# Pooled attention and a gated feed-forward net: the odd 64 query rows of two heads share one pass of the product with v

## The chip, the cores and the metric

The kernel runs on one core of a Trainium2 chip. A core has a matrix engine (PE, with its weight loads shown apart as PEld), a vector engine (DVE), an activation engine (ACT), a general engine (POOL) and a queue that issues transfers (SP). PE writes to a small accumulator memory (PSUM, eight banks of 512 float32 columns on 128 partitions); the other data lie in on-chip memory of 128 partitions. The metric is the device time of one execution in microseconds (us), lower is better; each of the times below is one execution.

## What is computed

There are 8 batches of 8 heads, 1152 keys and a head size of 64. Pairs of neighbouring query rows are averaged first, so a head has 576 query rows. The heads' outputs stand side by side as x (576 rows of 512 in a batch), and x goes through a net that mixes each row with the row before it:

```python
q_pool = q.reshape(B, H, S // 2, 2, D).mean(axis=3)
scores = scale * np.matmul(q_pool, k.transpose(0, 1, 3, 2))
scores = scores - np.max(scores, axis=-1, keepdims=True)
attn = np.exp(scores)
attn = attn / (np.sum(attn, axis=-1, keepdims=True) + 1e-09)
attn_out = np.matmul(attn, v)
# x: the heads side by side; x_prev: the row before, zeros ahead of the first
xk = mu_k * x + (1.0 - mu_k) * x_prev
xr = mu_r * x + (1.0 - mu_r) * x_prev
k = np.maximum(xk @ w_k, 0.0)          # 512 -> 1024
v = k * k @ w_v                        # 1024 -> 512
r = 1.0 / (1.0 + np.exp(-(xr @ w_r)))  # 512 -> 512
return r * v
```

The inputs are float32, the three weight matrices float64; the kernel splits numbers into a high and a low float16 part and sums products of the parts.

## The kernel before

**Attention.** A head's 576 query rows go in six blocks of 96 (`block`). For a block, nine PE products (L528) make the scores of 128 keys by 96 rows each in one of three PSUM buffers `s`; DVE takes the largest over the key chunks (`mx`, L535), PE turns it round (L538), DVE reduces it to one number per row (`mb`, L541), PE spreads its negative over a row (L543), and ACT writes that row, scaled a little up or down by its sign (Prelu), as row 96 of the low query parts (`qT`, L546). Nine more products (L552) then add the low parts and, through that row, subtract the maximum. ACT takes the exponential (`pf`, L558), an int32 whose upper half is the high part; POOL makes the low part from the lower half (`pl`, L566).

**The product with v.** `window` takes 128 of a head's rows as PE's stationary operand and v as the moving one: nine key chunks of `pf` against the parts of v (`vt`), then nine of `pl` (`vb`). 576 is four and a half times 128, so there are five windows per head, at rows 0, 128, 256, 352 and 448 (`WIN`), and the last ones overlap. Column 64 of v is ones, so that each result carries the row's sum. For the first 8 heads each chunk of `pf` meets the high and the low half of v in two products of 65 and 64 columns that add up in PSUM (L592, L594). From head 8 on (`SPLIT`) one product of 129 columns makes both halves side by side (L589), windows are taken out in two groups of three and two, and the halves are added afterwards: ACT copies one (`xlb`, L620), DVE adds it (L622). DVE also takes the sum (L615), its reciprocal (L617) and the scaled result (`xb`, L624). All of it lies in one PSUM bank, `a`, so the next group of windows begins when the one before it has been read. After every second head `xb` is turned round in five PE transposes (L636) and ACT copies it in two pieces to `xt` (L639).

**The net.** `ff` runs over tiles of 256 rows of x: mixing on ACT and DVE (L748, L751, L756, L759), then PE products of 256 or 512 columns (L780). The net of a batch can begin when its heads are done, so PE has it beside the attention of the next batch, and the last batch's net stands alone at the end. In the first batch there is no net yet; instead the weights are decoded on ACT, DVE and POOL (L657 to L691).

**What sets the order.** Every step is recorded as an `op` with engine, duration, what it reads and writes, and a key. `Issue` plays the steps through (list scheduling, with latencies `LAT`, `ISSUED`, `LANDED`), disturbs the priorities by a table of numbers (`MOVES`), and then issues them in the order found. On the chip each engine works through its own list in that order.

The lines of the change: `queries` loads and sums the query rows (L421, L423), `block` has the row of the maximum, `window` all of the product with v.

## Time and profile before

| | |
|---|---|
| median of three executions | 1159.55 us (1158.46 to 1159.95) |
| profiled execution, its own time | 1160.88 us |
| its span in the trace | 1159.1 us |
| granted PE clock, mean | 0.993 |
| busy: PE, DVE, ACT, POOL | 1115.5, 946.5, 917.6, 515.0 us |

The profile's page gives the busy time of each engine, 40 slices of the span, the chain of work that ended last and the costliest groups of instructions. A group's row names the line, the engine, the operation, output and inputs with their shapes, and how often it occurs; then the busy time, the mean of one in ns, and the idle time of the engine before it with what ended it. The timeline has one row for a run of equal instructions: start, length, and in brackets the idle time before it. A PE product's length counts from its start to its end in PSUM and overlaps with the next one's, so what a product occupies of PE is read from the distance of the starts. The view by windows gives the engines' busy time in a stretch of the span.

### The profile page before, as it was taken

To read this page: it belongs to the slowest core of one execution; us is meant where nothing else is said; L and a number is where in the kernel's file an instruction comes from. 1 tells how busy PE (TensorE), PEld (TensorE's weight loads), DVE (VectorE), ACT (ScalarE), POOL (GpSimd) and SP (SyncE) were. 2 spreads that over 40 slices of the span, in tenths; PEclk is the share of its full clock that TensorE was granted. 3 is DMA by queue.
4 is the path that set the end of the run, shared out by engine and by line. 5 is a ranking of instruction groups with operands and counts; after the bars stand their busy time and mean duration, and the time that the engine had idled before them with its cause. 6 is when DMAs were issued, how large, how long until landed. Compare 5 with 4: busy or idle time off the path is not lost.

```text
span 1159.1 us, 40985 instructions
## 1 busy us (share of the span) xinstructions
PE 1115.5 (96%) x17012; PEld 922.0 (80%) x17012; DVE 946.5 (82%) x2093; ACT 917.6 (79%) x1963; POOL 515.0 (44%) x541
## 2 busy tenths in 40 slices
PE   6787799999999999999999999999999999999998
PEld 5776787878788887988787888878797878788565
DVE  8888988889988979897888888887988987775531
ACT  7998897887878787887977877878888777866743
POOL 3555554644444444544444444445453544543111
PEclk9998899999999999999999999999999999999999
DMA  8877755553544434454454544354455433310000
GB/s 223 216 179 182 153 115 138 134 123 105 125 119 101 124 92 103 108 117 100 113 131 100 114 97 114 93 122 104 107 115 113 105 81 88 72 27 4 26 20 28
DMA packets 218667, 125.48 MB, mean 108 GB/s; under 512 B 153968, under 2 KB 190832, under 8 KB 218480
## 3 DMA queue, kind: packets, MB, share of 16 engines
q1 hardware_dynamic: 218480, 122.85, 44.9%
q8 instruction: 133, 2.18, 0.8%
q14 instruction: 54, 0.44, 0.1%
HBM read 67.11 MB, written 9.44 MB: 66 GB/s over the span
## 4 chain that ended last, share of the span: by engine, by line
PE 74%; ACT 7%; DVE 4%; issue 2%; DMA 0%; SPq 0%; ACTq 0%; DVEq 0%
PE f L780 30%; PE a L589 10%; PE s L528 9%; PE s L552 9%; PE a L599 5%; PE s L780 4%; ACT pf L558 2%; DVE mx L535 2%; PE a L780 2%; PE s L538 2%; PE a L636 1%; PE s L543 1%; ACT qT L546 1%; ACT qn L426 1%; ACT kn L474 0%
## 5 line engine op out<-in xcount | busy, mean ns | idle before, releaser
L566 POOL TENSOR_SCALAR pl<-pf 128x864 f16<-128x864 uint16 x384 | 374.1, 974 | 472.0 <-ACT pf L558 445.2
L535 DVE TENSOR_REDUCE mx<-s 128x96 f16<-128x864 f32 x384 | 400.8, 1052 | 69.2 <-PE s L528 40.7
L558 ACT ACTIVATE pf<-s 128x864 int32<-128x864 f32 x384 | 337.5, 891 | 70.2 <-PE s L552 45.7
L528 PE MATMUL s<-qT,ks 128*128 128x96 f16 x3456 | 225.0, 208 | 11.5 <-ACT pf L558 9.9
L528 PEld LDWEIGHTS <-ks 128*128 128x128 f16 x3456 | 189.9, 99 | 43.9 <-issue 19.4
L552 PE MATMUL s<-qT,ks 128*128 128x96 f16 x3456 | 218.9, 207 | 3.2 <-ACT qT L546 2.1
L589 PE MATMUL a<-vt,pf 128*128 128x129 f16 x2520 | 210.9, 220 | 0.5 <-DVE xb L624 0.5
L552 PEld LDWEIGHTS <-ks 128*128 128x128 f16 x3456 | 184.6, 99 | 26.9 <-issue 6.3
L589 PEld LDWEIGHTS <-pf 128*128 128x128 f16 x2520 | 159.6, 98 | 10.8 <-issue 0.6
L599 PE MATMUL a<-vb,pl 128*128 128x65 f16 x2880 | 151.2, 193 | 0.0
L546 ACT ACTIVATE qT<-s 1x96 f16<-1x96 f32 x384 | 92.0, 243 | 69.5 <-PE s L543 59.9
L780 PE MATMUL f<-xhk,wk_hi 128*128 128x256 f16 x496 | 135.1, 272 | 0.3 <-ACT r L807 0.3
L780 PE MATMUL f<-xhk,wk_lo 128*128 128x256 f16 x496 | 135.1, 272 | 0.0
L780 PE MATMUL f<-xlk,wk_hi 128*128 128x256 f16 x496 | 135.1, 272 | 0.0
L599 PEld LDWEIGHTS <-pl 128*128 128x128 f16 x2880 | 124.7, 98 | 3.6 <-POOL pl L566 0.2
L541 DVE TENSOR_REDUCE mb<-s 96x1 f16<-96x128 f32 x384 | 107.2, 282 | 22.9 <-PE s L538 18.9
L811 POOL TENSOR_TENSOR gl<-g 128x512 f16<-128x512 f32 x72 | 77.9, 1082 | 107.9 <-ACT g L809 105.2
L780 PEld LDWEIGHTS <-wk_hi 128*128 128x128 f16 x1152 | 107.0, 98 | 11.3 <-issue 0.4
L780 PE MATMUL f<-wv_hi,g 128*128 128x512 f16 x240 | 90.9, 379 | 0.9 <-ACT ex L828 0.7
L538 PE MATMUL s<-identb,mx 128*96 128x128 f16 x384 | 86.1, 226 | 5.4 <-DVE mx L535 5.2
L780 PE MATMUL f<-wv_hi,gl 128*128 128x512 f16 x240 | 90.9, 379 | 0.0
L780 PE MATMUL f<-wv_lo,g 128*128 128x512 f16 x240 | 90.9, 379 | 0.0
(106 smaller groups left out, 1976.9 us busy)
## 6 DMA issues: line engine op xcount, KB each, us to landing
kr<-in_k_dram SPq DMA_DIRECT2D x64, 288.0 KB, 3.0
vr<-in_v_dram SPq DMA_DIRECT2D x64, 288.0 KB, 3.0
qr<-in_q_dram SPq DMA_DIRECT2D x31, 320.0 KB, 3.6
ks<-ks SPq DMA_DIRECT2D x64, 144.0 KB, 2.8
out_dram<-em SPq DMA_DIRECT2D x36, 256.0 KB, 2.5
qr<-in_q_dram SPq DMA_DIRECT2D x32, 256.0 KB, 3.3
st<-in_moe_w_k_dram SPq DMA_DIRECT2D x8, 512.0 KB, 4.9
st<-in_moe_w_v_dram SPq DMA_DIRECT2D x8, 512.0 KB, 4.1
```

The source lines that it names most:

```text
L528: nc.tensor.matmul(cols(c, c + 1), ks1[hp][:, c, :], qhi, start=(c == c0), stop=False, skip_group_check=True)
L535: op("DVE", 0.975, lambda: nc.vector.tensor_reduce(mxz, grid(0, NC).rearrange("p c q -> p q c"), axis=AX.X, op=ALU.max), r=[("s", z)], w=[ ...
L538: op("PE", 0.059, lambda: nc.tensor.matmul(s[0:QN, 0:P], mxz, identb, start=False, stop=False, skip_group_check=True), r=[("mx", z)], w=[( ...
L541: op("DVE", 0.199, lambda: nc.vector.tensor_reduce(mbz[0:QN], s[0:QN, 0:P], axis=AX.X, op=ALU.max), r=[("s", z)], w=[("mb", z)], key=t + O ...
L546: op("ACT", 0.153, lambda: nc.scalar.activation(qlo[QN:QN + 1], s[QN:QN + 1, 0:QN], AF.Prelu, scale=1.0 - EPS, alpha=(1.0 + EPS) / (1.0 - ...
L552: nc.tensor.matmul(cols(c, c + 1), ks2[hp][:, c, :], qlo, start=False, stop=True, skip_group_check=True)
L558: op("ACT", NC * QN / 1200 + 0.06, lambda: nc.scalar.activation(pf[:, :, rows], grid(0, NC), AF.Exp, bias=SHIFT, scale=0.125 / (2.0 * SQ)) ...
L566: op(pe, d, lambda: en.tensor_scalar(pl[:, :, rows], half(pf, U16, 0)[:, :, rows], LO, 1.0, op0=ALU.mult, op1=ALU.mult), r=[("pf", j)], w= ...
L589: nc.tensor.matmul(bank[:, a0:a0 + VN + D], half(pf, F16, 1)[:, c, rows], vt[jv][:, c, 0:VN + D], start=(w == k0 and c == 0), stop=False, ...
L599: nc.tensor.matmul(bank[:, a0 + two * D:a0 + two * D + VN], pl[:, c, rows], vb[jv][:, c, 0:VN], start=False, stop=(c == NC - 1), skip_grou ...
L780: nc.tensor.matmul(ps, terms[i][0], terms[i][1], start=(first and i == 0), stop=(i == last), skip_group_check=True)
L811: op("POOL", 2 * n * 0.00203 + 0.08, lambda f2=f2: nc.gpsimd.tensor_tensor(gl[:, f2, 0:n], g32[:, f2, 0:n], gh[:, f2, 0:n], op=ALU.subtrac ...
```

## The change

The query rows of two neighbouring heads (an even one and the odd one after it) are laid out anew: the first 64 rows of both lie in one shared chunk, and the other 512 rows of each head make four windows of 128 without overlap. The exponentials of the even head's 64 rows lie at the end of `pf` and `pl` (which grow by 64), those of the odd head at the beginning. A new function `halves` runs once per two heads: for each chunk two products whose stationary operand has only 64 columns, one writing partitions 0 to 63 of bank `a` (even head, its v) and one partitions 64 to 127 (odd head, its v); the program gives them PE tiles of 128 rows by 64 columns at column 0 and column 64. Whole windows always use the two products that add up in PSUM, so the 129-column form, `SPLIT` and the copy and add per group of windows are gone; they remain for the shared pass alone. A head's windows are taken out together, four for the even head, four and the shared pass for the odd one. POOL copies the odd head's part of the shared result beside the even one's; the transposed results go to `xt` in four ACT copies, two of them of 64 columns on 64 partitions.

The row of the maximum becomes two rows: ACT writes Relu(x) and Relu(-x) with a scale that is a column of numbers (`sign`), and rows 96 and 97 of `ks2` hold the two factors; `EPS` doubles. DVE makes `sign` and `lift` and scales the two `ks2` at the start; POOL makes `negd`, which only a variant that isn't chosen (`row == "D"`) uses. The queries of two heads come in one transfer more. The planner's table `MOVES`, its seed's spread, some latencies and loads are other ones, so the order differs everywhere.

```diff
-EPS = 2.0 ** -10
+EPS = 2.0 ** -9
+ROW, ROW_N = "AA", 0
...
-SPLIT = 8
+HALF = 1.1
...
-    5, 10, 11, 17, 73, 89, 126, 158, 244, 307, 353, 431, 520, 523, 545, 560, 575, 593, 721, 784, 789, 846,
...
+    12, 57, 71, 78, 82, 116, 127, 165, 204, 389, 459, 497, 555, 573, 765, 911, 920, 1257, 1370, 1565, 1944,
...
-    LAT = {("PE", "DMA"): 1.46, ("PE", "PE"): 0.0,
+    LAT = {("PE", "DMA"): 0.2, ("PE", "PE"): 0.0,
...
-    ISSUED, LANDED, AHEAD = 1.44, 0.52, 8.0
+    ISSUED, LANDED, AHEAD = 1.2, 0.45, 8.0
...
-        return self.LAT.get((a, b), 1.22 if b == "DMA" else 0.18)
+        return self.LAT.get((a, b), 0.14 if b == "DMA" else 0.18)
...
-    WIN = [(0, 1), (128, 2), (256, 3), (352, 4), (448, 5)]
-    NW = len(WIN)
-    TURN = [(0, 3, 0), (3, 5, 384)]
+    HW, U = P // 2, 32
+    DONE = ((1, 2, 3, 5), (1, 3, 4, 5))
+    NW = 1 + len(DONE[0])
+    TURN = [(0, 3), (3, NW)]
+    SPAN = [(0, HW), (0, HW), (HW, HW + 2 * P), (HW + 2 * P, TQ)]
...
+    sign, lift = const.tile([P, 1], F32, name="sign"), const.tile([P, 1], F32, name="lift")
+    for c_, a_, b_ in ((sign, -2.0, 1.0), (lift, -2.0 * SM, SM * (1.0 - EPS))):
+        nc.vector.tensor_scalar(c_, ident[:, QN + 1:QN + 2], a_, b_, op0=ALU.mult, op1=ALU.add)
...
-        nc.vector.memset(t_[QN:QN + 1], SM)
+        nc.vector.memset(t_[QN:QN + 2], 1.0)
+        nc.vector.tensor_scalar(t_[QN:QN + 2], t_[QN:QN + 2], lift[QN:QN + 2], None, op0=ALU.mult)
...
-        op("ACT", 0.153, lambda: nc.scalar.activation(qlo[QN:QN + 1], s[QN:QN + 1, 0:QN], AF.Prelu,
-                                                      scale=1.0 - EPS, alpha=(1.0 + EPS) / (1.0 - EPS)),
-           r=[("s", z)] + kl, w=qm, key=t + O_MAX)
...
+                op("ACT", 0.267, lambda: nc.scalar.activation(qlo[QN:QN + 2], s[QN:QN + 2, 0:QN], AF.Relu,
+                                                              scale=sign[QN:QN + 2]),
+                   r=[("s", z)] + kl, w=qm, key=t + O_MAX)
...
+    def halves(n, t):
...
+        def both(r0, tb, c, vs, x0, x1, **kw):
+            for z, p0 in ((0, TQ), (1, 0)):
+                nc.tensor.matmul(a_b[z * HW:(z + 1) * HW, x0:x1], tb[:, c, p0:p0 + HW], vs[(n - 1 + z) % NV][:, c, r0:r0 + x1 - x0],
+                                 skip_group_check=True, **kw)
+
+        def mms():
+            for c in range(NC):
+                both(0, half(pf, F16, 1), c, vt, 0, place(0) + VN, start=(c == 0), stop=False)
+            for c in range(NC):
+                both(0, pl, c, vb, place(0), place(0) + VN, start=False, stop=(c == NC - 1))
...
+        x_ = xl_b[0]
+        op("ACT", 0.051 + D / 1200, lambda: nc.scalar.copy(x_, a_b[:, 0:D]), r=[ka], w=[("xlb",)], key=t + O_EVAC)
+        op("DVE", 0.07 + D / 960, lambda: nc.vector.tensor_tensor(
+            a_b[:, D:2 * D], a_b[:, D:2 * D], x_, op=ALU.add), r=[ka, ("xlb",)], w=[ka], key=t + O_EVAC)
...
-                if two:
-                    nc.tensor.matmul(bank[:, a0:a0 + VN + D], half(pf, F16, 1)[:, c, rows], vt[jv][:, c, 0:VN + D],
-                                     start=(w == k0 and c == 0), stop=False, skip_group_check=True)
-                    continue
...
+        op("POOL", 0.2, lambda: nc.gpsimd.tensor_copy(xb[0][:, 0, 0], xb[0][:, 0, 1]), r=[("xb", 1, 0)], w=[("xb", 0, 0)],
+           key=t + O_EVAC)
...
+            if j == 0 and n % 2:
+                halves(n, i * PER + O_AV)
+            for w, after in enumerate(DONE[n % 2]):
                 if after == j:
-                    window(n, w, i * PER + O_AV)
+                    window(n, w + 1, i * PER + O_AV)
```

How the program's order changes is seen at three places. The first is PE's list where a window of a head after the eighth goes over from the `pf` chunks to the `pl` chunks (`vt`, `vb`: the parts of v; `a`: the bank), before:

```order
L589 LDWEIGHTS pf
L589 MATMUL a<-vt_85,pf 128x129
L589 LDWEIGHTS pf
L589 MATMUL a<-vt_85,pf 128x129
L599 LDWEIGHTS pl
L599 MATMUL a<-vb_88,pl 128x65
```

and the same place of a window now:

```order
L656 LDWEIGHTS pf
L656 MATMUL a<-vt_87,pf 128x65
L658 LDWEIGHTS pf
L658 MATMUL a<-vt_87,pf 128x64
L663 LDWEIGHTS pl
L663 MATMUL a<-vb_90,pl 128x65
```

A `pf` chunk that had one load and one product now has two of each; the `pl` chunk is as it was. The second place is the shared pass, which has no counterpart before, at the same passage:

```order
L627 LDWEIGHTS pf
L627 MATMUL a<-vt_86,pf 64x129
L627 LDWEIGHTS pf
L627 MATMUL a<-vt_87,pf 64x129
L627 LDWEIGHTS pl
L627 MATMUL a<-vb_89,pl 64x65
L627 LDWEIGHTS pl
L627 MATMUL a<-vb_90,pl 64x65
```

The two heads' products (`vt_86` and `vt_87`) take turns, 18 with `pf` and 18 with `pl`, and nothing of other work stands between them. The third place is POOL's list in the second half of a batch, before:

```order
L566 TENSOR_SCALAR pl<-pf 128x9x96
L811 TENSOR_TENSOR gl_114<-g_0_113 128x512
L501 TENSOR_SCALAR vb_89<-vr_73 128x9x64
L811 TENSOR_TENSOR gl_114<-g_0_113 128x512
L566 TENSOR_SCALAR pl<-pf 128x9x96
```

and now, with the copy (L687) that each two heads' transposes wait for:

```order
L520 TENSOR_SCALAR vb_89<-vr_72 128x9x64
L606 TENSOR_SCALAR pl<-pf 128x9x96
L687 COPY xb_104<-xb_104 128x64
L873 TENSOR_TENSOR gl_117<-g_0_116 128x512
L606 TENSOR_SCALAR pl<-pf 128x9x96
```

The copy stands behind a `pl` of the same queue, which itself waits for an exponential; a `gl` of the net and the next `pl` stand behind the copy.

More of the change, by code (lines that the diff above doesn't have):

```diff
@@ L442, in queries @@
                     qT[i][:, r_, js], qn[0][:, r_, js].rearrange("p j x -> p (j x)")),
[L443 removed]
+                   r=[(m, c) for c in jk], w=[(t_, i, c) for c in jk], key=key + 2, load=0.155 * (j1 - j0))
     def turn16(src, bank, kb, r, dst, w, eng, key):
@@ L516, in block @@
         s = s_b[z]
-        rows = slice(j * QN, (j + 1) * QN)
-        mxz, mbz = mx[z], mb[z]
+        p0 = (0 if hp else HW) + j * QN
+        rows, us = slice(p0, p0 + QN), range(p0 // U, (p0 + QN) // U)
+        mxz, mbz, mtz = mx[z], mb[z], mt[z]
+        row = ROW[int(n >= ROW_N)]
         def cols(c0, c1):
@@ new lines, in block, with lower @@
+        if row == "D":
+            def lower(c0, c1):
+                for c in range(c0, c1):
+                    nc.tensor.matmul(cols(c, c + 1), mbz[0:QN].broadcast_to([QN, P]), negd[0:QN, 0:QN],
+                                     start=False, stop=False, skip_group_check=True)
+            op("PE", NC * 0.0430, lambda: lower(0, NC), r=[("mb", z)], w=[("s", z)], key=t + O_MAX)
+        else:
+            op("PE", 0.047, lambda: nc.tensor.matmul(s[:, 0:QN], mbz[0:QN].broadcast_to([QN, P]),
+                                                     negi[0:QN, 0:QN], start=False, stop=False, skip_group_check=True),
+               r=[("mb", z)], w=[("s", z)], key=t + O_MAX)
+            if row == "A":
+                op("ACT", 0.267, lambda: nc.scalar.activation(qlo[QN:QN + 2], s[QN:QN + 2, 0:QN], AF.Relu,
+                                                              scale=sign[QN:QN + 2]),
+                   r=[("s", z)] + kl, w=qm, key=t + O_MAX)
+            else:
+                op("ACT", 0.175, lambda: nc.scalar.copy(qlo[QN:QN + 1], s[QN:QN + 1, 0:QN]),
+                   r=[("s", z)] + kl, w=qm, key=t + O_MAX)
@@ L562, in block @@
             op(pe, NC * QN / 1200 + 0.09, lambda: nc.scalar.activation(
-                pl[:, :, rows], half(pf, U16, 0)[:, :, rows], AF.Copy, scale=LO), r=[("pf", j)], w=[("pl", j)], key=t + O_REST)
+                pl[:, :, rows], half(pf, U16, 0)[:, :, rows], AF.Copy, scale=LO), r=[("pf", x) for x in us], w=[("pl", x) for x in us], key=t + O_REST)
         else:
@@ L614, in window @@
-        xk = [("xb", hh, x[0]) for x in TURN if k0 <= x[0] < k1]
-        op("DVE", 0.075, lambda: nc.vector.tensor_scalar(dz, u[:, :, d0 + D], GUARD, None, op0=ALU.add),
-           r=[ka], w=[("den", z, k0)], key=t + O_EVAC)
-        op("DVE", 0.08, lambda: nc.vector.reciprocal(dz, dz), r=[("den", z, k0)], w=[("den", z, k0)], key=t + O_EVAC)
-        if two:
-            xl_ = xl_b[0][:, 0:k1 - k0]
-            op("ACT", 0.051 + (k1 - k0) * D / 1200, lambda: nc.scalar.copy(xl_, u[:, :, 0:D]),
-               r=[ka], w=[("xlb",)], key=t + O_EVAC)
-            op("DVE", 0.07 + (k1 - k0) * D / 960, lambda: nc.vector.tensor_tensor(
-                u[:, :, D:2 * D], u[:, :, D:2 * D], xl_, op=ALU.add), r=[ka, ("xlb",)], w=[ka], key=t + O_EVAC)
@@ L624, in window @@
-        op("DVE", 0.07 + (k1 - k0) * D / 960, lambda: nc.vector.tensor_tensor(
-            xz[:, :, hh], u[:, :, d0:d0 + D], dz.unsqueeze(2).broadcast_to([P, k1 - k0, D]), op=ALU.mult),
-           r=[("den", z, k0), ka], w=xk, key=t + O_EVAC)
-        if hh == 0 or w < NW - 1:
+        k0, z = 1 - hh, n % 2
+        nk = NW - k0
+        u = bank[:, place(k0):place(NW)].rearrange("p (k x) -> p k x", x=VN)
+        dz = den[z][:, k0:NW]
+        op("DVE", 0.075, lambda: nc.vector.tensor_scalar(dz, u[:, :, D], GUARD, None, op0=ALU.add),
+           r=[ka], w=[("den", z)], key=t + O_EVAC)
@@ L628, in window @@
+        op("DVE", 0.08, lambda: nc.vector.reciprocal(dz, dz), r=[("den", z)], w=[("den", z)], key=t + O_EVAC)
+        op("DVE", 0.07 + nk * D / 960, lambda: nc.vector.tensor_tensor(
+            xb[0][:, k0:NW, hh], u[:, :, 0:D], dz.unsqueeze(2).broadcast_to([P, nk, D]), op=ALU.mult),
+           r=[("den", z), ka], w=[("xb", hh, x[0]) for x in TURN], key=t + O_EVAC)
+        if hh == 0:
             return
-        for t0, t1, q0 in TURN:
-            base = WIN[t0][0]
-            qe = WIN[t1 - 1][0] + P
-            def turned(t0=t0, t1=t1, base=base):
+        op("POOL", 0.2, lambda: nc.gpsimd.tensor_copy(xb[0][:, 0, 0], xb[0][:, 0, 1]), r=[("xb", 1, 0)], w=[("xb", 0, 0)],
+           key=t + O_EVAC)
```

115 lines of the change are left out of this document (69 added, 46 removed), and 14 rows, old and new, of the table AHEAD2.

## The prediction

> **What bounds the kernel now.** I read the view by windows first, over three stretches: the first batch, the batches that have a net beside them, and the net alone.
>
> ```profile
> core 0: us, PE busy (x) PEld busy (x) DVE busy (x) ACT busy (x) POOL busy (x), PEclk, DMA share, GB/s
> 0.00:155.00 155.00, 121.31 (x2403) 109.30 (x2404) 137.32 (x281) 136.79 (x272) 80.68 (x89) 0.94 0.76 186
> 155.00:1070.00 915.00, 909.01 (x14080) 760.80 (x14079) 779.11 (x1754) 736.10 (x1595) 421.35 (x440) 1.00 0.45 103
> 1070.00:1159.00 89.00, 85.16 (x533) 51.92 (x531) 30.11 (x59) 44.70 (x97) 12.98 (x12) 1.00 0.07 25
> ```
>
> The middle stretch is PE's: 909.01 of 915 us busy, so 6.0 us are free. In the first 155 us PE is free for 33.7 us, while DVE and ACT are busy for 137 each. Busy PE isn't yet full PE, since lengths overlap, so I then read starts in the timeline of PE.
>
> ```profile
> 464.23 0.67 PE L589 MATMUL a<-vt,pf 128*128 128x129 f16 x9
> 464.74 0.44 PE L599 MATMUL a<-vb,pl 128*128 128x65 f16 x9
> 465.02 0.55 PE L552 MATMUL s<-qT,ks 128*128 128x96 f16 x9
> 465.40 0.33 PE L589 MATMUL a<-vt,pf 128*128 128x129 f16 x3
> ```
>
> Each row starts where the one before leaves room: nine products of 129 columns occupy 464.74 - 464.23 = 0.51 us (57 ns each), nine of 65 occupy 0.28 (31 ns), nine of 96 occupy 0.38. So PE is filled product to product, and work taken from PE here should shorten the span one for one. The chain of waits agrees, with three quarters of the span on PE:
>
> ```profile
> PE 74%; ACT 7%; DVE 4%; issue 2%; DMA 0%; SPq 0%; ACTq 0%; DVEq 0%
> ```
>
> The rule I use: the change in time is the change of PE's work after 155 us, plus what the first stretch gets longer or shorter, plus new holes in PE's list.
>
> **Term 1, PE's work per two heads.** Heads 0 to 7 lie in the first stretch, where PE has room; 56 heads, 28 pairs, count. Before, a pair has ten windows of 0.51 + 0.28 = 0.79, that is 7.90 us. Now it has eight windows in the two-product form, which the first eight heads already use:
>
> ```profile
> 63.63 0.19 PE L592 MATMUL a<-vt,pf 128*128 128x65 f16 x1
> 63.66 0.19 PE L594 MATMUL a<-vt,pf 128*128 128x64 f16 x1
> ...
> 64.15 0.19 PE L594 MATMUL a<-vt,pf 128*128 128x64 f16 x1
> 64.17 0.44 PE L599 MATMUL a<-vb,pl 128*128 128x65 f16 x9
> ```
>
> Nine chunks take 64.17 - 63.63 = 0.54, so a window takes 0.82 and eight take 6.56. The shared pass, 18 products of 129 columns and 18 of 65, is in no trace. Call it X; the pair changes by X - 1.34. If both column tiles work at once, X is one window's 0.79 and 28 pairs give -15.4 us. If they work one after the other, X is two windows' 1.58 and 28 pairs give +6.7. In between lie the weight loads, 36 of 64 columns. The nearest rows:
>
> ```profile
> L538 PEld LDWEIGHTS <-mx 128*96 128x96 f16 x384 | 47.4, 124 | 17.2 <-DVE mx L535 9.5
> L599 PEld LDWEIGHTS <-pl 128*128 128x128 f16 x2880 | 124.7, 98 | 3.6 <-POOL pl L566 0.2
> ```
>
> The only load that isn't 128 columns wide has fewer columns and takes 26 ns more, so a narrow load is slower per column. If a column of it costs what a moving column costs (57 ns / 129 = 0.44 ns), 64 columns take 28 ns, and 36 loads one after the other, behind products that overlap in twos, make X = 1.0. I take that: -0.34 x 28 = -9.5 us, with -15.4 and +6.7 kept as ends.
>
> The Trainium skill speaks against the change here: "TensorEngine Tiling (Array Packing)", section Restrictions, says that column tiling disables the fast weight load, and "TensorE: Matmul & The Clock Gate", section LDWEIGHTS, prices a plain load at its columns divided by 1.2 GHz. By that figure, as an estimate, 64 columns take 53 ns, 36 loads 1.9 us, and the term would be +16 us instead of -9.5. The same figure would set a plain load of 96 columns 53 ns above a fast one of 128, where the two rows above show 26, so I hold with half of it; no run here shows a load on a column tile.
>
> **Term 2, ACT.** The Relu reads its scale from a column of numbers. The trace has the same kind of step with and without one:
>
> ```profile
> L748 ACT ACTIVATE tmp<-xt,omu_k 128x256 f32<-128x256 f32 x48 | 24.2, 508 | 1.0 <-DVE xm L751 0.6
> L756 ACT CAST xhk<-xm 128x256 f16<-128x256 f32 x72 | 27.6, 402 | 3.4 <-PE s L780 1.8 <-PE f L780 0.8 <-DVE xm L751 0.7
> L546 ACT ACTIVATE qT<-s 1x96 f16<-1x96 f32 x384 | 92.0, 243 | 69.5 <-PE s L543 59.9 <-DVE ex L835 1.0 <-DVE den L615 0.5
> ```
>
> That is 106 ns more, so the step goes from 243 to about 350 ns, a second row on another partition costing nothing of its own. The copies:
>
> ```profile
> L639 ACT COPY xt<-a 128x384 f32<-128x384 f32 x32 | 15.4, 481 | 4.0 <-PE a L636 3.4 <-DVE mx L535 0.3
> L639 ACT COPY xt<-a 128x192 f32<-128x192 f32 x32 | 10.2, 319 | 2.3 <-PE a L636 1.8 <-PE s L543 0.2
> L620 ACT COPY xlb<-a 128x192 f32<-128x192 f32 x56 | 17.8, 318 | 6.2 <-DVE den L615 3.9 <-PE a L599 1.5
> L620 ACT COPY xlb<-a 128x128 f32<-128x128 f32 x56 | 14.9, 265 | 7.6 <-DVE den L615 6.3 <-ACT vt L491 0.3
> ```
>
> They fit 0.16 us and 0.83 ns per column, so 64 columns take 0.21 and 256 take 0.37. Per pair the copies to `xt` go from 0.80 to 2 x 0.21 + 2 x 0.37 = 1.16. The copies of halves go from 2 x 0.58 to 0.21 in the middle, and from none to 0.21 in the first stretch. With the number of maximum rows by stretch,
>
> ```profile
> 14.00:155.00 141.00, 13.20 (x57) 0.94 0.75 179
> 155.00:1070.00 915.00, 78.61 (x327) 1.00 0.45 103
> ```
>
> the middle gets 327 x 0.106 + 28 x (0.36 - 0.95) = +18 us of ACT: 754 of 915, still under PE, so nothing. The first stretch gets 57 x 0.106 + 4 x 0.57 = +8.3 us, into 18.2 us that ACT has free there. There PE is what waits, and this is for what:
>
> ```profile
> PE s L528 <- ACT pf L558: 8.9, 20, 1.0
> ```
>
> 8.9 of the 33.7 us that PE is free there are put down to ACT's exponential, a quarter; I let a third of 8.3 through, +3 us, with ends 0 and +8.3.
>
> **Term 3, the start on DVE.** `sign`, `lift` and two scalings of 2 x 1152 numbers come ahead of the copy of the first turned keys.
>
> ```profile
> 2.36 1.02 DVE L404 MEMSET ks<- 1x1152 f16 x1 [0.30 <-DVE ks L403]
> 7.23 0.42 DVE L459 COPY ks<-s 128x512 f16<-128x512 f16 x1 [0.89 <-ACT ks L456]
> ```
>
> Filling 1152 numbers takes 1.02 us; two scalings and two small steps are some 2.3. They fall into the 0.89 us that DVE waits there and delay the rest by up to 1.4. I take +1, ends 0 and +2.3.
>
> **What costs nothing, and its cover.** DVE loses the add and one of two take-outs per head:
>
> ```profile
> L622 DVE TENSOR_TENSOR a<-a,xlb 128x192 f32<-128x192 f32 x56 | 19.9, 355 | 4.4 <-ACT xlb L620 3.7
> L624 DVE TENSOR_TENSOR xb<-a,den 128x192 f32<-128x192 f32 x56 | 19.6, 350 | 0.7
> L622 DVE TENSOR_TENSOR a<-a,xlb 128x128 f32<-128x128 f32 x56 | 16.4, 293 | 5.9 <-ACT xlb L620 4.4
> L624 DVE TENSOR_TENSOR xb<-a,den 128x128 f32<-128x128 f32 x56 | 15.9, 284 | 0.8
> L617 DVE RECIPROCAL den<-den 128x3 f32<-128x3 f32 x56 | 9.4, 167 | 0.5
> L615 DVE TENSOR_SCALAR den<-a 128x2 f32<-128x2 f32 x56 | 8.8, 158 | 14.1 <-PE a L599 8.3 <-ACT xlb L620 4.9
> ```
>
> Two sums and two reciprocals (0.65), the adds (0.65) and the scalings (0.63) make 1.93 us per head; now one sum and one reciprocal (0.33), a scaling of 256 or 320 columns (about 0.45) and half an add of 64 (0.11) make 0.89. The 58 us saved on DVE over 56 heads lie beside PE's 909 and are worth at most a part of PE's 6.0 free us. The copy on POOL is smaller than its 0.97 us neighbour `pl`; behind it stand `gl` and `pl`, and the transposes wait for it. In PE's new list 27 scoring products (three times 0.38) and eleven products of the net stand between the last window of an odd head and its transposes, against a sum, reciprocal, scaling and copy of some 1.1 us; without that cover it would cost up to 1.1 x 32. The extra query transfer waits for the same free buffer as its neighbours on SP. The shorter transfer latencies only matter where the planner places a use just behind a landing:
>
> ```profile
> qT<-qn SPq DMA_TRANSPOSE x64, 3.6
> ks<-kn SPq DMA_TRANSPOSE x62, 3.3
> ```
>
> The new constants promise 1.2 + 1.4 + 0.45 = 3.05 for the second, 0.25 less than the median. The new order as a whole I set at 0, ends -6 (PE's free time in the middle) and +6.
>
> **Sum.** -9.5 + 3 + 1 = -5.5. Against the profiled execution's own 1160.88 (span 1159.1 and 1.8 around it) that is 1155.4; that execution lies 1.3 above the median of the runs shown, so I forecast 1154.1 for the median.
>
> **The rivals.**
>
> *The tiles overlap fully* (X = 0.79, loads hidden): -15.4, with +2 in the first stretch 1146. For it: the two tiles have their own columns and partitions, and at 98 ns the present loads vanish behind products 31 ns apart. Against: the slower narrow load.
>
> *The first stretch takes the gain back.* All of the 8.3 us on ACT and 1 to 2 at the start pass through, -9.5 + 9.8: 1159.9, no change. For it: DVE and ACT are both at 137 of 155. Against: PE's waits there name ACT for only a quarter.
>
> *The array empties at each change between whole and tiled columns.* A 65-column product lasts 193 ns and the next starts 31 behind it:
>
> ```profile
> L599 PE MATMUL a<-vb,pl 128*128 128x65 f16 x2880 | 151.2, 193 | 0.0
> ```
>
> Emptying costs 0.16 us, going in and coming out 0.32 per pair, so X = 1.32, term 1 is -0.6 and with +4 the end is 1163, slower. It decides from X = 1.2 on, where term 1 no longer pays for the 4 us of terms 2 and 3. The Trainium skill has this as a rule ("TensorEngine Tiling (Array Packing)", section Key Properties: changing the tiling mode drains the engine); all products of the trace are of one mode, so no run here shows it.
>
> *The tiles work in turn* (X = 1.58): +6.7 + 4, 1170, slower. That the change does not reach the chip as tiles is part of this: the program's list gives outputs of 64 partitions, but a list doesn't show overlap.
>
> **How the numbers follow.** The forecast (X from 0.9 to 1.15, ends 1148 to 1160) has 0.42, full overlap 0.17, the gain taken back 0.16, emptying 0.13, turns 0.12. A measurement of this kernel can tell about 0.2% (2.3 us) from no change. Faster: 0.33 of the forecast's 0.42, the 0.17 and 0.04 of the third, 0.54. Same: 0.08 of the forecast, 0.10 of the third and 0.01 of the fourth, 0.19. Slower: the rest, 0.27. The forecast's own range is 1148 to 1160; to hold 8 in 10 it goes down to 1143 (full overlap with some of PE's 6 free us) and up to 1167 (emptying, and the better part of turns).
>
> **What would show each step.** Eight windows: two products per chunk, 30 ns from start to start, nine chunks 0.54. The pass: from its first product to the next work's start 1.0 us, its loads about 112 ns long; 0.79, 1.3 or 1.6 would be the rivals'. The Relu at 350 ns, and PE's free time in the first stretch, where the net's first products should begin some 4 us later. `xlb` 32 instead of 112 times. PE still busy for 99% of the middle. I would be wrong if the middle had holes before L692 (POOL's copy late) or before L549 (keys late), or if X were above 1.2.

## The result

| | before | changed |
|---|---|---|
| median | 1159.75 us (1158.46 to 1161.77, 4 runs) | 1175.84 us (1174.95 to 1177.35, 4 runs) |
| profiled execution, its span | 1160.88, 1159.1 | 1174.95, 1173.2 |
| busy: PE, DVE, ACT, POOL | 1115.5, 946.5, 917.6, 515.0 | 1116.6, 900.7, 947.3, 527.5 |

The kernel became slower: a ratio of 1.0138, 95% interval 1.012 to 1.0157, some 16 us, above the upper end of the range (1167). The view by windows of the changed kernel, cut where the net begins and where it stands alone:

```profile
0.00:155.00 155.00, 117.67 (x2284) 104.91 (x2285) 131.68 (x274) 138.91 (x270) 80.27 (x91) 0.90 0.80 178
155.00:1085.00 930.00, 914.52 (x16148) 756.35 (x16146) 739.87 (x1518) 763.06 (x1581) 434.22 (x471) 1.00 0.48 103
1085.00:1173.20 88.20, 84.45 (x530) 51.50 (x528) 29.17 (x58) 45.33 (x97) 12.99 (x12) 1.00 0.06 23
```

The middle takes 930 instead of 915 us, and PE still counts as 98% busy. The column hides the cause, since products overlap. So I went through the starts of all products, counted each at the usual distance from a start of its kind to the next (57 ns for 129 columns, 42 for 96 and so on), and called the rest of the distance free (the some 9 us that are left of each span lie ahead of the first product and behind the start of the last; the split between work and free moves by a few us with the distances taken):

```
                      before    changed   p1 (below)
work, whole span      1068.5    1049.6    1049.6
free, whole span        81.3     114.5      95.8
  of it up to 155 us    55.6      63.9      59.1
  of it in the middle   25.4      50.4      36.4
span                  1159.1    1173.2    1154.4
```

PE did lose 18.9 us of work, and it gained 33.2 us of holes. The holes are what this study is about. The profile puts only part of them down to a wait. Waits of PE between 160 and 1060 us (total, times, longest), first before, then changed:

```profile
PE s L543 <- DVE mb L541: 1.4, 3, 0.7
PE s L528 <- ACT pf L558: 1.0, 5, 0.3
PE s L552 <- ACT qT L546: 0.2, 1, 0.2
```

```profile
PE s L549 <- ACT pf L598: 5.4, 12, 1.4
PE s L592 <- ACT qT L583: 4.0, 6, 1.4
```

Both new waits are for ACT: for the exponential that frees a buffer `s`, and for the row of the maximum. This is the pass of the product with v in the timeline of the changed kernel (start, length), and its loads among the groups, above the load of 96 columns:

```profile
499.59 0.70 PE L627 MATMUL a<-vt,pf 128*64 128x129 f16 x18
500.13 0.45 PE L627 MATMUL a<-vb,pl 128*64 128x65 f16 x18
500.51 0.34 PE L549 MATMUL s<-qT,ks 128*128 128x96 f16 x4
```

```profile
L627 PEld LDWEIGHTS <-pf 128*64 128x64 f16 x576 | 17.8, 112 | 4.2 <-issue 2.2
L559 PEld LDWEIGHTS <-mx 128*96 128x96 f16 x384 | 47.7, 125 | 16.8 <-DVE mx L556 8.8
```

From its first product to the next work the pass takes 500.51 - 499.59 = 0.92 us. And these are the steps of ACT and POOL that the change touches:

```profile
L583 ACT ACTIVATE qT<-s,sign 2x96 f16<-2x96 f32 x384 | 124.7, 332 | 71.5 <-PE s L579 56.9 <-DVE mb L563 2.9 <-DVE xm L813 2.0
L639 ACT COPY xlb<-a 128x64 f32<-128x64 f32 x32 | 6.8, 211 | 2.8 <-PE a L627 2.5
L702 ACT COPY xt<-a 128x256 f32<-128x256 f32 x64 | 23.7, 370 | 1.3 <-PE a L692 0.5
L702 ACT COPY xt<-a 64x64 f32<-64x64 f32 x64 | 13.2, 206 | 7.6 <-PE a L692 6.8
L687 POOL COPY xb<-xb 128x64 f32<-128x64 f32 x32 | 14.1, 442 | 18.9 <-DVE xb L682 18.0
```

### The profile page after: what moved, and what is told of

The parts are those of the page before. It is cut to its first block, busy times and chain, and to the rows that moved or that the text cites. A ratio compares the mean times of both kernels' runs of the same rounds, so it can differ in the third digit from the quotient of the medians.

```text
span 1173.2 us, 44732 instructions
## 1 busy us (share of the span) xinstructions
PE 1116.6 (95%) x18956; PEld 912.8 (78%) x18956; DVE 900.7 (77%) x1849; ACT 947.3 (81%) x1947; POOL 527.5 (45%) x574
## 4 chain that ended last, share of the span: by engine, by line
PE 73%; ACT 12%; DMA 6%; DVE 5%; issue 4%; SPq 0%; ACTq 0%; DVEq 0%
PE f L842 27%; PE s L549 11%; PE s L592 10%; PE a L658 5%; PE a L656 5%; PE a L663 5%; ACT pf L598 4%; PE s L842 4%; DMA ks<-kn 4%; DVE mx L556 2%; ACT qT L583 2%; PE a L627 2%; PE s L559 2%; PE a L842 2%; PE s L579 1%
## 5 line engine op out<-in xcount | busy, mean ns | idle before, releaser
L549 PE MATMUL s<-qT,ks 128*128 128x96 f16 x3456 | 222.4, 208 | 22.6 <-ACT pf L598 18.0
L549 PEld LDWEIGHTS <-ks 128*128 128x128 f16 x3456 | 188.8, 99 | 58.0 <-issue 32.2
L592 PE MATMUL s<-qT,ks 128*128 128x96 f16 x3456 | 214.4, 208 | 12.4 <-ACT qT L583 10.7
L592 PEld LDWEIGHTS <-ks 128*128 128x128 f16 x3456 | 182.4, 99 | 38.7 <-issue 19.0
L656 PE MATMUL a<-vt,pf 128*128 128x65 f16 x2304 | 196.0, 194 | 1.0 <-DVE a L640 0.6
L658 PE MATMUL a<-vt,pf 128*128 128x64 f16 x2304 | 196.3, 195 | 0.0
L583 ACT ACTIVATE qT<-s,sign 2x96 f16<-2x96 f32 x384 | 124.7, 332 | 71.5 <-PE s L579 56.9
L656 PEld LDWEIGHTS <-pf 128*128 128x128 f16 x2304 | 164.9, 99 | 5.2 <-ACT pf L598 0.5
L658 PEld LDWEIGHTS <-pf 128*128 128x128 f16 x2304 | 157.4, 98 | 7.6 <-issue 1.5
L873 POOL TENSOR_TENSOR gl<-g 128x512 f16<-128x512 f32 x72 | 78.6, 1093 | 107.3 <-ACT g L871 104.4
L663 PE MATMUL a<-vb,pl 128*128 128x65 f16 x2304 | 122.8, 194 | 0.1
L663 PEld LDWEIGHTS <-pl 128*128 128x128 f16 x2304 | 97.6, 98 | 4.4 <-POOL pl L606 0.3
```

The lines of the kernel that those rows point to most:

```text
L549: nc.tensor.matmul(cols(c, c + 1), ks1[hp][:, c, :], qhi, start=(c == c0), stop=False, skip_group_check=True)
L583: op("ACT", 0.267, lambda: nc.scalar.activation(qlo[QN:QN + 2], s[QN:QN + 2, 0:QN], AF.Relu, scale=sign[QN:QN + 2]), r=[("s", z)] + kl, w= ...
L592: nc.tensor.matmul(cols(c, c + 1), ks2[hp][:, c, :], qlo, start=False, stop=True, skip_group_check=True)
L656: nc.tensor.matmul(bank[:, a0:a0 + VN], half(pf, F16, 1)[:, c, rows], vt[jv][:, c, D:D + VN], start=(w == 1 and c == 0 and hh == 0), stop= ...
L658: nc.tensor.matmul(bank[:, a0:a0 + D], half(pf, F16, 1)[:, c, rows], vt[jv][:, c, 0:D], start=False, stop=False, skip_group_check=True)
L663: nc.tensor.matmul(bank[:, a0:a0 + VN], pl[:, c, rows], vb[jv][:, c, 0:VN], start=False, stop=(c == NC - 1), skip_group_check=True)
```

## The experiments

Three explanations stood against each other after the result: R, the Relu whose scale is a column of numbers; T, the new table with the shorter transfer latencies, which lets uses stand too early in the lists; and O, that the new order is a worse one in itself. After the first four experiments came B, the chain of a block (scores, maximum, row, scores, exponential) that goes through three buffers `s` and sets the pace whatever PE has to do, against W, the prediction's own rule; the last ones set A, ACT's list as a whole, against K, a block's chain alone. Unless said otherwise an experiment keeps the order of its starting kernel in every engine's list and differs in the shown lines alone. Differences from p1 are those of the medians; the median of the kernel before, run beside each group, stayed between 1158.9 and 1161.0. With both intervals such a difference is uncertain by some 2.5 us. The diffs show the instruction without the `op(...)` around it.

**p1: the changed kernel with the old row of the maximum** (the factor `1.0 - EPS` is already in `ks2`, so the scale here is 1.0).

```diff
-activation(qlo[QN:QN + 2], s[QN:QN + 2, 0:QN], AF.Relu, scale=sign[QN:QN + 2])
+activation(qlo[QN:QN + 1], s[QN:QN + 1, 0:QN], AF.Prelu, scale=1.0, alpha=(1.0 + EPS) / (1.0 - EPS))
```

> The changed kernel with the one-row Prelu back (constant scale) and every engine's list as in the changed kernel; the results are the same ones. Theory R (the Relu's 332 ns instead of 243 ns in each block's chain lets PE run dry before the second scores and, a buffer later, before the first): the step returns to about 243 ns, the holes before L592 shrink to the 4 us of the kernel before and about 12 to 18 us come back, 1158 to 1164 us. Theory T (the shorter transfer latencies put work behind landings that come later): at most 4 us come back, 1172 to 1176. Theory O (the order itself is a worse one): 2 to 8 us come back, the 0.1 us of ACT per block in the first 155 us alone, 1168 to 1174.

1158.08 us against 1160.38, ratio 0.9979 (0.9964 to 0.9994). The one step accounts for the whole loss: 1175.84 - 1158.08 = 17.8 us, and what is left of the change is a gain that can just be told from none. p1 keeps the new order, so O is refuted too. The groups and the middle stretch of p1:

```profile
L583 ACT ACTIVATE qT<-s 1x96 f16<-1x96 f32 x384 | 90.6, 242 | 77.5 <-PE s L579 60.6 <-DVE mb L563 2.8 <-DVE xm L813 2.0
...
155.00:1065.00 910.00, 898.66 (x16051) 748.95 (x16046) 744.16 (x1507) 723.20 (x1570) 432.80 (x469) 1.00 0.48 105
```

The step is 332 - 242 = 90 ns shorter; from its start to the next ACT instruction's, where that one waits for nothing, it is 267 instead of 357. 384 times 90 ns are 34.6 us of ACT, of which 17.8 reach the end. The net's first product comes at 144.2 us (before 144.6, changed 149.2), so 5 of them lie in the first stretch.

**p2 and p3: the order.** p2 is the changed kernel with an empty table; p3 besides has the latencies and transfer durations of the kernel before. Here the lists do differ.

```diff
-MOVES, BASE, REACH = (
-    12, 57, 71, 78, 82, 116, 127, 165, 204, 389, 459, 497, 555, 573, 765, 911, 920, 1257, 1370, 1565, 1944,
...
-), 3000000, 1150.0
+MOVES, BASE, REACH = (), 0, 1150.0
```

```diff
-LAT = {("PE", "DMA"): 0.2, ("PE", "PE"): 0.0,
+LAT = {("PE", "DMA"): 1.46, ("PE", "PE"): 0.0,
...
-ISSUED, LANDED, AHEAD = 1.2, 0.45, 8.0
+ISSUED, LANDED, AHEAD = 1.44, 0.52, 8.0
...
-return self.LAT.get((a, b), 0.14 if b == "DMA" else 0.18)
+return self.LAT.get((a, b), 1.22 if b == "DMA" else 0.18)
```

> The changed kernel with an empty table of moves, so that the order is the planner's own under the new latencies. A reference for the next run. Theory R: within 6 us of the changed kernel, 1170 to 1182. Theory T: as slow or slower, 1175 to 1190, with ACT waiting for the key transposes (L493 behind ks<-kn) as much as now (15 us in the middle). Theory O: it can land on either side, 1165 to 1185, since only the table made the order special.

> The same without the table, but with the transfer latencies and loads of the kernel before in the planner. Theory T: faster than the run with the new ones by 8 us or more, and ACT's wait for the key transposes falls from 15 us to under 5. Theories R and O: within 4 us of the run with the new ones.

1177.0 us (ratio 1.014, 1.0124 to 1.0155) and 1174.99 (1.0127, 1.0098 to 1.0156). The wait that T names is there. ACT's waits for turned keys in the middle, of the changed kernel, p2 and p3:

```profile
ACT kn L493 <- DMA ks<-kn: 15.2, 19, 2.2
```

```profile
ACT kn L486 <- DMA ks<-kn: 9.8, 11, 2.0
```

```profile
ACT kn L486 <- DMA ks<-kn: 2.6, 3, 1.0
```

It falls from 15.2 to 2.6 us, and the time by 2 at most. T is refuted as a cause of the 16 us, and what the new table is worth, some 1 us (p2 against the changed kernel), can't be told from nothing.

**b1: the kernel before with the Relu of two rows alone**, with its `sign`, `lift` and scaled `ks2` at the start.

```diff
-activation(qlo[QN:QN + 1], s[QN:QN + 1, 0:QN], AF.Prelu, scale=1.0 - EPS, alpha=(1.0 + EPS) / (1.0 - EPS))
+activation(qlo[QN:QN + 2], s[QN:QN + 2, 0:QN], AF.Relu, scale=sign[QN:QN + 2])
```

> The kernel before, with the Relu of two rows and its start-up steps in place of the Prelu, and the rest of every list in the same order. Theory R: the Relu alone costs what the changed kernel lost beside its gain, 12 to 20 us, 1172 to 1180. Theories T and O: the first stretch alone gets longer, by the 3 to 6 us of the prediction's terms 2 and 3, 1163 to 1166.

1189.08 us, ratio 1.025 (1.0234 to 1.0267): +28.7, more than the 12 to 20 that R gave. Up to some 5 us of it can be the start-up steps', which p1 and the changed kernel both have: the net's first product comes at 149.8 us here and at 144.6 before.

```profile
L550 ACT ACTIVATE qT<-s,sign 2x96 f16<-2x96 f32 x384 | 126.3, 333 | 64.9 <-PE s L547 55.3 <-DVE xlk L763 0.6 <-DVE den L619 0.4
...
155.00:1098.00 943.00, 926.97 (x14171) 767.64 (x14168) 781.81 (x1764) 779.73 (x1608) 424.97 (x444) 1.00 0.44 101
```

The same step, the same 333 ns, and 0.83 of ACT's 34.6 us come out at the end, against 0.51 between p1 and the changed kernel. ACT is busy 780 of 943 us here and was 736 of 915 before: there was free time in plenty, but not where the lists put the step.

**r1: the changed kernel with a constant as the Relu's scale**, one execution. The second row then repeats the first instead of holding Relu(-x).

```diff
-AF.Relu, scale=sign[QN:QN + 2])
+AF.Relu, scale=1.0)
```

> The changed kernel with the Relu of two rows, but a constant scale in place of the column of numbers (the second row then repeats the first, and the maximum is wrong for negative numbers). If the column is what makes the step longer, its 332 ns fall to about 243 and the time to about 1158; if the second row or the Relu does, it stays at 332 and at 1175.

1158.68 us, within p1's executions (1152.7 to 1161.1).

```profile
L583 ACT ACTIVATE qT<-s 2x96 f16<-2x96 f32 x384 | 90.9, 242 | 77.3 <-PE s L579 63.6 <-DVE mb L563 2.8 <-DVE xm L813 2.0
```

Two rows with Relu take the 242 ns of one row with Prelu. What costs 90 ns is the column of numbers, neither the function nor the row.

**s1: p1 with the two tiles in turn.** The pass lists the 18 products of the even head, then those of the odd one.

```diff
-            for c in range(NC):
-                both(0, half(pf, F16, 1), c, vt, 0, place(0) + VN, start=(c == 0), stop=False)
-            for c in range(NC):
-                both(0, pl, c, vb, place(0), place(0) + VN, start=False, stop=(c == NC - 1))
+            for z, p0 in ((0, TQ), (1, 0)):
+                for c, lo in [(c, lo) for lo in (0, 1) for c in range(NC)]:
+                    one(z, p0, 0, pl if lo else half(pf, F16, 1), c, vb if lo else vt, place(0) if lo else 0, place(0) + VN,
+                        start=(c == 0 and not lo), stop=bool(c == NC - 1 and lo))
```

> The changed kernel with the Prelu, in which the shared pass does all 18 products of the even head and then all 18 of the odd head instead of taking turns; every other list is as it was. In the changed kernel the pass's products start in pairs 2 ns apart. Theory P (two neighbours on different column tiles run at once): without neighbours on different tiles the pass goes from 0.92 to about 1.7 us from its first product to the next work. Theory W (PE's work sets the pace of the middle, one for one): 28 times 0.77 us longer than the run with the Prelu alone, +20 us, 1178. Theory B (the three score buffers set it together with PE): about half of that or less, +5 to +12, 1163 to 1170.

1175.55 us, ratio 1.0131 (1.0112 to 1.015). The timeline of PE in s1:

```profile
495.99 0.70 PE L627 MATMUL a<-vt,pf 128*64 128x129 f16 x9
496.53 0.35 PE L627 MATMUL a<-vb,pl 128*64 128x65 f16 x6
...
496.83 0.56 PE L627 MATMUL a<-vt,pf 128*64 128x129 f16 x7
497.23 0.45 PE L627 MATMUL a<-vb,pl 128*64 128x65 f16 x9
497.61 0.34 PE L549 MATMUL s<-qT,ks 128*128 128x96 f16 x4
```

Nine products on one tile take 496.53 - 495.99 = 0.54 us; in the changed kernel eighteen on two tiles took the same 0.54. So the tiles work at once. The pass takes 1.615 us instead of 0.918 (medians of the 32), 28 of them in the middle are 19.5 us of PE work added, and 17.5 come out at the end, 0.9 of them: near the 20 that W gave, and more than B's 5 to 12.

**d1 and b2: PE work taken away.** In the last whole window of each head seven of the nine `pl` products are left out, in d1 from p1, in b2 from the kernel before.

```diff
-            for c in range(c0, c1):
+            for c in range(c0, c1) if w < NW - 1 else (c1 - 1,):
```

> The changed kernel with the Prelu, leaving out seven of nine products with the low parts in the last window of each head (the result lacks them); all other lists are the same. PE loses 7 x 30 ns = 0.21 us per head, 11.8 us over 56 heads. Theory W: 11 to 13 us faster than the run with the Prelu alone, 1145 to 1147. Theory B: 2 to 7 us faster, 1151 to 1156, with more idle time of PE.

> The kernel before, leaving out seven of nine products with the low parts in the last window of each head (the result lacks them), every list else the same: 0.21 us less of PE per head, 11.8 us over the 56 heads after the first stretch. The prediction's rule (in the middle PE's work counts one for one) asks for 11 to 13 us less, 1147 to 1149. If the rule was wrong for this kernel from the start, and not only for the changed order, it is a third of that, as in the changed kernel with the Prelu: 3 to 5 us less, 1155 to 1158.

7 x 30 ns x 56 heads are 11.8 us less PE work after the first stretch. d1 takes 1153.8 us, ratio 0.9944 (0.9928 to 0.9961), 4.3 below p1: 0.36 of it, within what B gave and a third of what W gave. b2 takes 1156.99 against 1158.94, ratio 0.9982 (0.9972 to 0.9991): 2.0, a sixth, and less than either alternative had it (11 to 13, or 3 to 5). The middle stretches, d1 and then b2:

```profile
155.00:1070.00 915.00, 899.38 (x15686) 742.19 (x15685) 747.10 (x1517) 730.63 (x1591) 433.12 (x469) 1.00 0.48 104
```

```profile
155.00:1070.00 915.00, 905.48 (x13752) 752.58 (x13749) 779.82 (x1761) 739.13 (x1604) 426.27 (x444) 1.00 0.46 104
```

b2 speaks to the kernel of the prediction itself: with PE counted as busy for 99% of the middle, taking 11.8 us from it shortened the time by 2.

**m1: p1 with the maximum over five of the nine key chunks**, so the subtracted number isn't always the largest.

```diff
-tensor_reduce(mxz, grid(0, NC).rearrange("p c q -> p q c"),
+tensor_reduce(mxz, grid(0, 5).rearrange("p c q -> p q c"),
```

> The changed kernel with the Prelu, where the largest score is taken over the first five of nine key chunks only (any number near the maximum cancels in the quotient, so the result hardly moves). DVE's step in each block's chain goes from 1.05 to about 0.6 us; PE has the same work. Theory W: only the first stretch gets shorter, 3 to 8 us, and the middle by the 5 us at most that PE waits visibly. Theory B: the score buffers come free earlier, the hold of 7.65 us per buffer falls to about 7.0 or less, PE's idle time in the middle (34 us by starts) mostly goes, and the run is 20 to 40 us faster, 1120 to 1140.

1153.76 us, ratio 0.9942 (0.9927 to 0.9958): 4.3 below p1, not the 20 to 40 that B gave.

```profile
L556 DVE TENSOR_REDUCE mx<-s 128x96 f16<-128x480 f32 x384 | 249.6, 655 | 129.6 <-PE s L549 91.2 <-PE s L579 10.3 <-ACT pf L598 7.9
L563 DVE TENSOR_REDUCE mb<-s 96x1 f16<-96x128 f32 x384 | 109.0, 286 | 108.9 <-PE s L559 99.6 <-PE s L579 5.7
```

The second of these groups in p1, and then in a2 below:

```profile
L563 DVE TENSOR_REDUCE mb<-s 96x1 f16<-96x128 f32 x384 | 107.3, 282 | 39.6 <-PE s L559 35.5 <-PE s L579 1.4
L563 DVE TENSOR_REDUCE mb<-s 96x1 f16<-96x128 f32 x768 | 217.7, 286 | 38.2 <-PE s L559 22.9 <-PE s L579 0.5
```

The maximum is 1052 - 655 = 397 ns shorter in each chain. But the turned maximum has a fixed place in PE's list and comes when it came before: `mb` waits 99.6 us for it instead of 35.5, and a buffer is held as long as in p1 (7.65 us on average after the first stretch, from the first score to the end of the exponential). So B is refuted in its plain form: the chain alone doesn't hold the pace either.

**a1, a2, a3: steps made longer and shorter, from p1.** a1 does ACT's copies of v (`vt`, L510), which are outside a block's chain, twice from head 8 on; a2 does the reduction `mb`, which is inside it, twice; a3 cuts the copies of v to one chunk.

```diff
-activation(vt[j][:, cs, D:2 * D], vr[i][:, cs], AF.Copy, scale=SV)
+[activation(vt[j][:, cs, D:2 * D], vr[i][:, cs], AF.Copy, scale=SV) for _ in range(2 if n >= 8 else 1)]
```

```diff
-tensor_reduce(mbz[0:QN], s[0:QN, 0:P], axis=AX.X, op=ALU.max)
+[tensor_reduce(mbz[0:QN], s[0:QN, 0:P], axis=AX.X, op=ALU.max) for _ in (0, 1)]
```

```diff
-activation(vt[j][:, cs, D:2 * D], vr[i][:, cs], AF.Copy, scale=SV)
+activation(*[x[:, slice(cs.stop - 1, cs.stop) if n >= 8 else cs] for x in (vt[j][:, :, D:2 * D], vr[i])],
+           AF.Copy, scale=SV)
```

> The changed kernel with the Prelu, in which ACT's scaled copies of v (vt, two per head, needed many blocks later) are done twice from head 8 on; all lists else the same. That is about 0.67 us more of ACT per head, 37 us over 56 heads, about what the Relu's column of numbers adds to ACT (384 times 0.09 = 35), but off each block's chain. Theory A (ACT's list itself is part of what sets the pace, whatever the work is): 10 to 18 us slower than the run with the Prelu, 1168 to 1176. Theory K (only the chain of a block, the three buffers' hold, counts): at most 4 us slower, 1158 to 1162.

> The same base, with DVE's reduction to one number per row (mb) done twice: 0.2 us more in each block's chain and 77 us more of DVE, nothing on ACT. Theory K: more than twice the Relu's effect, 25 us or more slower, 1183 and up. Theory A: 0 to 8 us slower, 1158 to 1166, since DVE has room (745 of 915 us busy in the middle).

> The same base, with ACT's scaled copies of v cut to one of five and one of four key chunks from head 8 on (the other chunks keep older numbers, so the result is not the reference's): about 0.37 us less of ACT per head, 21 us over 56 heads, off the chain. Theory A, if it holds in both directions: 5 to 10 us faster, 1148 to 1153. Theory K, or if PE and the chain hold the pace as soon as ACT gives way: 0 to 3 us faster.

a1: 1185.24 us, ratio 1.0207 (1.0192 to 1.0223), 27 above p1. a2: 1200.17, 1.0338 (1.0317 to 1.0359), 42 above p1. a3: 1155.69, 0.9953 (0.9937 to 0.997), 2.4 below p1 for 21 us less of ACT. What a1 and a2 added is more than foretold, 50 us of ACT instead of 37 and 110 of DVE instead of 77 (217.7 against 107.3): a step done again on the same output starts only when the first has ended, 0.315 us after its start for `mb`, where another step follows after 0.20. Neither theory holds alone: a1 refutes K (at most 4) and goes beyond A (10 to 18), a2 refutes A (0 to 8) and fits K (25 or more), and a3's 2.4 is within K's 0 to 3. PE's waits between 160 and 1060 us in p1 and a1, and (to 1085) in a2:

```profile
PE s L549 <- ACT pf L598: 3.8, 7, 1.4
PE s L592 <- ACT qT L583: 2.8, 4, 1.3
```

```profile
PE s L549 <- ACT pf L598: 14.6, 27, 1.3
PE s L592 <- ACT qT L583: 12.0, 23, 1.2
```

```profile
PE s L579 <- DVE mb L563: 12.2, 31, 1.1
PE s L549 <- ACT pf L598: 3.4, 6, 1.0
```

In a1 no step of the chain got longer, and yet PE's waits for the exponential and for the row rise from 6.6 to 26.6 us, 20 of the 27 lost: those two steps stand behind the longer copies in ACT's list. In a2 the wait appears at the step that was made longer.

Together, per us of work added to or taken from one engine, in fixed lists:

| | engine, us of work | time | share that arrives |
|---|---|---|---|
| b1 (Relu, order of before) | ACT +34.6 | +28.7 | 0.83 |
| changed against p1 (Relu) | ACT +34.6 | +17.8 | 0.51 |
| a1 | ACT +50 | +27 | 0.54 |
| a2 | DVE +110 | +42 | 0.38 |
| s1 | PE +19.5 | +17.5 | 0.90 |
| d1 | PE -11.8 | -4.3 | 0.36 |
| b2 | PE -11.8 | -2.0 | 0.17 |
| m1 | DVE -152 | -4.3 | 0.03 |
| a3 | ACT -21 | -2.4 | 0.11 |

The small shares are uncertain by half of themselves or more (d1: 4.3 with some 2.5 either way; b2, against the kernel beside it: 2.0 with 1.1). On each engine the work that was added arrives by more than the work that was left out: PE 0.90 against 0.36 and 0.17, ACT 0.51 to 0.83 against 0.11, DVE 0.38 against 0.03. But these are different steps at different places, and it isn't the sign alone: seen from the changed kernel p1 leaves ACT work out, and half of it arrives. No engine alone is the bound, though one of them counts as 99% busy.

**Where the holes end.** PE's starts tell more than its waits. This is a place in the changed kernel, first PE, then ACT:

```profile
504.87 0.21 PE L579 MATMUL s<-negi,mb 96*128 96x96 f16 x1
...
506.09 0.20 PE L658 MATMUL a<-vt,pf 128*128 128x64 f16 x1
506.26 0.54 PE L592 MATMUL s<-qT,ks 128*128 128x96 f16 x9
```

```profile
504.47 0.87 ACT L598 ACTIVATE pf<-s 128x864 int32<-128x864 f32 x1
505.24 0.62 ACT L895 ACTIVATE em<-em 128x512 f32<-128x512 f32 x1
505.88 0.33 ACT L583 ACTIVATE qT<-s,sign 2x96 f16<-2x96 f32 x1
```

The second scores (L592) start 0.17 us after the product before them, where 0.03 is usual, and the view counts no idle time, since that product is 0.20 us long. They start 0.05 us after the row (L583) has ended. The row's input from PE (L579) was there at 505.08, but ACT was at an exponential and a step of the net until 505.86.

I did the same for every block. Its first scores (L549, in the kernel before L528) need the exponential of three blocks earlier, which frees their buffer, and its second ones (L592, L552) its own row; in no block do they start sooner than 50 ns after the end of that ACT step. Counted are the holes of more than 20 ns in the middle that end at most 60 ns after it, in us (of the scores that start without such a hole, at most 5% lie as close):

| | behind the exponential | behind the row | together |
|---|---|---|---|
| before | 7.2 | 3.4 | 10.6 |
| b2 | 10.4 | 5.9 | 16.3 |
| b1 | 15.1 | 13.3 | 28.4 |
| p1 | 7.2 | 4.6 | 11.8 |
| s1 | 5.7 | 3.5 | 9.2 |
| d1 | 12.0 | 6.8 | 18.8 |
| changed | 14.4 | 10.2 | 24.6 |
| a1 | 19.1 | 18.1 | 37.2 |

From p1 to the changed kernel these holes grow by 12.8 us, of the 14.0 by which all holes of the middle grow, and from p1 to a1 by 25.4 of the 27 us lost. For 93% or more of each sum ACT had been idle for less than 30 ns, or not at all, ahead of the step: PE was waiting for a step that stood behind others in ACT's list. In a1 it is the copies of v that stand right ahead for 16.9 us of the sum, against 0.4 in p1. Where PE's work was left out the holes grow too, by 7.0 us in d1 and 5.7 in b2 of the 11.8 taken away, and where PE's work was added (s1) they shrink by only 2.6. (The profiled execution of b2, 1161.4 us, lies above its median, but its middle is the part counted here.)

## Why the prediction was wrong

Two steps failed: the rule, which promised that PE's saving arrives, and Term 2's "so nothing" for the Relu. Of the 21.7 us between the forecast (1154.1) and the result, the Relu's 17.8 less the some 2 foretold for it in the first stretch make some 16, and the saving that didn't arrive makes some 5.

**The rule (one for one with PE's work) failed.** It was read from the windows and from products that follow each other without room. Both rows were right, but the conclusion wasn't: in this kernel, before any change, 11.8 us of PE work were worth 2 us (b2). Of PE's 25 us of holes in the middle, short ones that the busy column hides, 10.6 end with an exponential or a row that PE needs and that stood behind other steps in ACT's list; with less PE work they get longer (16.3 us in b2). In p1 PE does 18.9 us less than before, of which 13 are left after some 6 for going in and out of the tiled columns (below), and the time fell by 2.3.

**Term 1 (X = 1.0) came out in size, not in kind, and so by luck.** The pass takes 0.918 us from its first product on, and some 0.09 more ahead of it, so X is 1.01, where full overlap would be 0.79 and turns 1.58 (s1 with the same counting: 1.7). I had put the 0.2 above full overlap down to the narrow loads. The load is 112 ns long as estimated, but it hides: nine pairs with `pf` take 0.54 us, 60 ns each where the 129 columns alone take 57. What costs lies at the two borders of the pass: from the start of a scoring product (L592) to the pass's first product go 136 ns where 43 are usual, and from the last pair to the next work 125 where 30 are. That is 0.09 to 0.10 us each way, 0.19 per pass. So the rival in which the array empties had its extra time, at 0.1 instead of 0.16 each way (whether by emptying, or by loads that can't run ahead at the border, these runs don't tell apart), and X stayed below the 1.2 from which it decides. The Trainium skill's rule that changing the tiling mode drains the engine ("TensorEngine Tiling (Array Packing)", section Key Properties) agrees with these two distances. Its price for a plain load, 53 ns for 64 columns ("TensorE: Matmul & The Clock Gate", section LDWEIGHTS), doesn't: in s1 products of 65 columns on one tile, each with a load of its own, start 30 ns apart. The prediction's 1.9 us had all 36 loads one after the other; 18 on each of two tiles at work at once would by that price fill 0.96, as an estimate, close to the 0.92 measured, so s1 decides here and not the pass. Its reason for holding with half of that price doesn't stand either: 53 ns between a plain load of 96 columns (80 by that price) and a fast one of 128 takes the fast one to be 27 ns, which no row shows.

**Term 2 failed at its cheapest line**, "+18 us of ACT … still under PE, so nothing". The Relu's duration was right (350 foretold, 332 measured), and so were the copies (0.21 and 0.37 us; 206 and 370 ns). The cover was wrong. I compared ACT's busy sum, 754 of 915, with PE's, as if any free time of ACT could take the work. The row of the maximum stands between two score products that PE's list has at fixed places, and whatever is behind it on ACT, exponentials above all, moves back with it: the holes of PE that end with one of these two steps grow from 11.8 us in p1 to 24.6. r1 and p1 show that this one operand cost 17.8 us, 5 of them in the first stretch and some 13 in the middle, where I had written nothing.

**The first stretch and the start** (+3 and +1) were about right: the net's first product comes at 149.2 instead of 144.6 us, +4.6, and at 144.2 with the old row, so it goes away with the Relu, while the start on DVE, which p1 keeps, wasn't seen by itself. The granted clock there was 0.90 in the changed kernel and 0.94 before, but the clock isn't needed for the 4.6 us: b1 had 0.96 there and its net began 5.2 us late, and p2 had 0.93 and took 1177 us in all.

**What I let cost nothing.** DVE's busy time fell from 946.5 to 900.7 us, 46 where I had 58, and together with all the rest that brought the 2.3 us of p1; m1 shows what a further 152 are worth (4.3). POOL's copy took 0.44 us of the 0.97 allowed, and in the middle no wait of PE is put down to it. The transfer latencies did make waits (15.2 us of ACT), worth 2 us at most. The order's ends of -6 to +6 can't be read apart from the rest, since too much else is in p1's gain.

**The rivals.** The gain taken back by the first stretch alone would have ended at 1159.9; the first stretch took its 4.6, but the middle lost more. None of the rivals had the loss where it was, since each took the rule for granted and varied PE's work or the first stretch only. A rival that began "ACT's row comes 90 ns later 384 times, in a chain that PE's list waits for" would have had 35 us as its upper end, and was open to be written from the same row.

**What stays open.** The list of waits shows little of this: from p1 to the changed kernel the two named waits only grow from 6.6 to 9.4 us, since a scoring product is 208 ns long and the next may start 42 behind it, so a hole of up to 0.17 us disappears under the last product's length. The starts show it, for the middle; for the first stretch, which lost 5 of the 17.8, they weren't gone through in this way. Why half of the Relu's 34.6 us arrives, and not a tenth or all, isn't worked out. DVE's part (m1, a2) wasn't gone through by starts either. Whether a new order, found with the measured 357 ns for the row and 1.01 us for the pass, would win back more wasn't tried. That b1 pays more (0.83) than the changed kernel (0.51) fits with their orders having been made for a row of 0.153 and of 0.267 us, but the two orders differ in much else, so this too is only argued. The one version that beats both kernels is p1, by 0.2%.

## What to carry to other kernels

Where a column of busy time says that one engine is full, read its holes from the starts of its products, and see which engine's step ends just ahead of them. Where several engines work through fixed lists and none is free for long, measure the worth of a saving before building it: leave a little work out and duplicate a little, and see what share arrives, for the two shares can be 0.36 and 0.90 on the same engine in the same kernel. A free fifth of an engine is no cover for a step that another engine's list waits for; ask how often the step occurs and who stands behind it, and don't cost it at nothing: here a third to nearly all of what was added arrived. When a change carries a side edit (here the row of the maximum), time the side edit by itself: the pass, with all else that came along, was worth 2 us and its companion cost 18.
